# Block-sparse attention and a gated feed-forward on one core: a list-scheduled order, q and k turned by DMA transposes, and a first batch cut into units of 128, 256 and 384 tokens

## The chip, the cores and the metric

The kernel runs on one core of one Trainium2 chip. Times are device microseconds of that core. Every result below is the median of the runs of one kernel, and each was timed against the kernel before in the same rounds on the same chip. One core has no second die to compare with, so a run counts as slow only if it lies more than 1.5% above the fastest of its kernel.

TensorE does the matrix products, VectorE and ScalarE the elementwise work, GpSimd some small work and the loads that change the type on the way, SyncE issues other transfers. A transfer is issued on the queue of one engine and carried out by 16 DMA engines that all queues share.

## The reference

```python
# attention: q, k, v are (4 batches, 8 heads, 768 tokens, 64), float32
scores = scale * np.matmul(q, k.transpose(0, 1, 3, 2))
mask = ...                       # 24 x 24 blocks of 32: window, first and last block, 3 sampled
scores = np.where(mask, scores, -1000000000.0)
attn = softmax(scores)           # cut
x = np.matmul(attn, v)           # then to (3072 tokens, 512)
# feed-forward
xn = x / np.sqrt(np.mean(x * x, axis=-1, keepdims=True) + 1e-06) * rms_g
g, val = xn @ w_gate, xn @ w_val          # 512 -> 1536
out = (g * sigmoid(g) * val) @ w_out      # 1536 -> 512
```

## The kernel before

The mask is added inside the score product. A score tile is the product of 88 rows: 64 of the head, and 24 that select a block of 32 keys and carry the block mask. So `X` holds q and k transposed, with 24 mask rows below them. A pair of heads is one slot of `X`; four pairs make a batch, and each batch is two units of 384 tokens.

```python
    def load_qk(b, lo, hi):                       # casts float32 to bfloat16 on the way
        ...
        nc.gpsimd.dma_start(out=qraw[b][:, lo:hi, :], in_=qv[b, :, lo:hi, :])
        nc.gpsimd.dma_start(out=kraw[b][:, lo:hi, :], in_=kv[b, :, lo:hi, :])

    def transposes(b, pr, early=False):           # 24 for a pair, on TensorE
        ...
        for i, src in enumerate((qraw[b], kraw[b])):
            for c in range(NC):
                for h in range(2):
                    nc.tensor.transpose(
                        out=tt[i][64 * h:64 * h + 64, c * P:(c + 1) * P],
                        in_=src[:, 2 * pr + h, c * D:(c + 1) * D], identity=ident)
        for h in range(2):                        # out of PSUM, on VectorE
            ...
                nc.vector.tensor_copy(
                    out=X[0:D, sl, h], in_=t_[64 * h:64 * h + 64, :, 0:S])

    def ff_g(u, f, wide):                         # gp has one PSUM buffer
        ...
            gp = ps_f.tile([P, TG], FP32, name="gp", tag="gp")
        for c in range(NP):
            nc.tensor.matmul(out=gp, lhsT=wg[...], rhs=xns[u][:, c, :], ...)
        nc.scalar.activation(out=th, in_=gp, func=AF.Tanh, scale=0.5)
        nc.vector.scalar_tensor_tensor(           # uu = (th + 1) * gp frees gp
            out=uu, in0=th, scalar=1.0, in1=gp, op0=ALU.add, op1=ALU.mult)
```

The order of emission comes from a loop over steps. Each step issues one score product and its exp. Other work either has a fixed step or comes from a queue of feed-forward products, paid with credits. Every engine carries out its instructions in the order of emission.

The softmax here doesn't subtract the row's maximum and nothing guards it: scores larger than these inputs give would overflow.

## Time and profile before

| | before |
|---|---|
| median time | 372.5 us |
| TensorE busy | 326.6 us, 88% |
| first score product | 11.1 us |
| first gate product | 52.5 us |

These are lines of the profile's page. The rows of digits divide the span into 40 slices and give the busy tenths of each; PEclk is the clock granted to TensorE in tenths. The queue lines give packets, megabytes and the time that the packets took as a share of all 16 engines' span; q0 is GpSimd's queue, q1 SyncE's. The last two lines are the chain of waits that ended last.

```profile
span 371.2 us, 7228 instructions
...
PE 326.6 (88%) x3074; PEld 197.0 (53%) x3074; DVE 203.0 (55%) x369; ACT 221.8 (60%) x358; POOL 27.4 (7%) x42
...
PE   2768689977989789988999889998999799989995
...
PEclk9999859999999999999999999999999999999999
DMA  6999998006000090006000000000000000000012
...
DMA packets 19877, 21.18 MB, mean 57 GB/s; under 512 B 772, under 2 KB 16644, under 8 KB 19844
...
q0 software_dynamic: 16208, 14.16, 24.6%
q1 hardware_dynamic: 3636, 6.56, 4.9%
...
PE 68%; ACT 15%; DVE 11%; DMA 2%; issue 2%; POOL 1%; DVEq 0%; POOLq 0%
PE gp L297 13%; PE yp L328 13%; PE vp L314 12%; ACT pt L225 6%; ACT sq L253 4%; ACT xn L282 3%; DVE xq L270 3%; DVE uu L303 2%; ACT th L301 2%; DVE X L179 2%; DVE X L182 2%; DMA kb<-in_k_dram 1%; PE tqk L173 1%; DMA out_dram<-yo 1%; PE gw L297 1%
```

TensorE is the limit: it has the most busy time, and 68% of the chain. It is poorly filled only in the first six slices. The DMA engines are nearly full there and almost free afterwards.

The timeline and the groups tell what q and k cost. Columns of the timeline are start, duration, engine, line, operation, output and inputs, count, and in brackets the idle time before it with what ended that. The groups give busy time and mean nanoseconds, then idle time before the group and what ended it.

```profile
6.41 0.85 PE L173 MATMUL tqk<-ident,qb 128*64 128x128 bf16 x12 [6.41 <-DMA qb<-in_q_dram]
...
8.28 1.92 DVE L182 COPY X<-tqk 64x1536 bf16<-64x1536 bf16 x2 [1.49 <-PE tqk L173]
...
11.14 0.82 PE L221 MATMUL s__182<-X 88*128 88x384 bf16 x2 [2.16 <-DVE X L187]
```

```profile
L182 DVE COPY X<-tqk 64x1536 bf16<-64x1536 bf16 x26 | 24.8, 953 | 4.7 <-PE tqk L173 4.5
...
L173 PE MATMUL tqk<-ident,qb 128*64 128x128 bf16 x156 | 7.2, 230 | 6.5 <-DMA qb<-in_q_dram 6.4
```

The first pair's q is in SBUF at 6.4 us and the first score product starts at 11.1 us. A pair costs TensorE 24 transposes at a pitch of 0.033 us, and VectorE two copies of 0.95 us. The Trainium skill (TensorE: Matmul & The Clock Gate, Part 4: PE-mode transpose) gives about 390 ns for a 128x128 transpose in isolation and 275 ns in one kernel. The trace shows less for one of these (230 ns, with 64 columns of the array and not 128), and they overlap: from the start of the first of 24 to the start of the next product it is 0.79 us, so 16 pairs cost 12.7 us and not the 88 that 384 durations of 230 ns would add up to.

In this document "lost" time of TensorE is the length of a window less the products in it times their pitch at full clock (0.1625 us for 128x384, 0.216 for 128x512, 0.033 for a q/k transpose, and so on). A product is counted once, in the window in which it starts, and time at a reduced clock counts as lost in part. Before, that leaves 31.5 us lost up to the first gate product, 11.4 from there to 125 us, 18.8 from 125 to 366, and 4.8 at the end.

### The profile page before, as it was taken

The page shows a single profiled execution, that of the slowest core. Times are in us where ns is not written, and L with a number is a line of the kernel's source. Part 1 is how long each engine was busy: PE and PEld are TensorE (multiplying, and loading weights), DVE is VectorE, ACT ScalarE, POOL GpSimd, SP SyncE. Part 2 cuts the span into 40 slices and gives each one's busy share as a digit, 9 for nine tenths or more (in the row PEclk, how much of TensorE's full clock was granted, in tenths as well). Part 3 has the DMA queues.
Part 4 walks back from the last instruction along what each step waited for, and adds up shares of the span by engine and source line. Part 5 has one row for each costly group of instructions (what it writes and reads, how often), then busy time and mean ns, then how long its engine had stood idle before and what let it go on. Part 6 is the DMA issues. An engine that isn't in the chain of part 4 may idle for free.

```text
span 371.2 us, 7228 instructions
## 1 busy us (share of the span) xinstructions
PE 326.6 (88%) x3074; PEld 197.0 (53%) x3074; DVE 203.0 (55%) x369; ACT 221.8 (60%) x358; POOL 27.4 (7%) x42
## 2 busy tenths in 40 slices
PE   2768689977989789988999889998999799989995
PEld 1345355654656456655666456655666466545552
DVE  4664225666575645655464645665554545476650
ACT  2638947686646756676666766576666866532211
POOL 8520200010000200001000000000000000000000
PEclk9999859999999999999999999999999999999999
DMA  6999998006000090006000000000000000000012
GB/s 95 170 210 208 204 207 129 2 2 87 0 30 30 3 195 4 28 32 86 28 30 4 26 14 18 28 30 3 29 30 29 1 30 28 2 28 31 28 59 86
DMA packets 19877, 21.18 MB, mean 57 GB/s; under 512 B 772, under 2 KB 16644, under 8 KB 19844
## 3 DMA queue, kind: packets, MB, share of 16 engines
q0 software_dynamic: 16208, 14.16, 24.6%
q1 hardware_dynamic: 3636, 6.56, 4.9%
q8 instruction: 24, 0.39, 0.4%
q14 instruction: 9, 0.07, 0.1%
HBM read 28.57 MB, written 6.29 MB: 94 GB/s over the span
## 4 chain that ended last, share of the span: by engine, by line
PE 68%; ACT 15%; DVE 11%; DMA 2%; issue 2%; POOL 1%; DVEq 0%; POOLq 0%
PE gp L297 13%; PE yp L328 13%; PE vp L314 12%; ACT pt L225 6%; ACT sq L253 4%; ACT xn L282 3%; DVE xq L270 3%; DVE uu L303 2%; ACT th L301 2%; DVE X L179 2%; DVE X L182 2%; DMA kb<-in_k_dram 1%; PE tqk L173 1%; DMA out_dram<-yo 1%; PE gw L297 1%
## 5 line engine op out<-in xcount | busy, mean ns | idle before, releaser
L303 DVE SCALAR_TENSOR_TENSOR uu<-th,gp 128x384 bf16<-128x384 bf16 x90 | 49.9, 554 | 82.8 <-ACT th L301 82.3
L297 PE MATMUL gp<-xn,wg 128*128 128x384 bf16 x360 | 73.9, 328 | 5.6 <-DVE uu L303 5.6
L328 PE MATMUL yp<-wo,hp 128*128 128x512 bf16 x288 | 75.9, 379 | 0.0
L314 PE MATMUL vp<-xn,wv 128*128 128x384 bf16 x360 | 73.3, 326 | 0.3 <-DVE hp L317 0.3
L301 ACT ACTIVATE th<-gp 128x384 bf16<-128x384 f32 x90 | 43.9, 487 | 35.9 <-PE gp L297 35.5
L221 PEld LDWEIGHTS <-X 88*128 88x128 bf16 x384 | 36.0, 101 | 43.0 <-issue 13.9
L297 PEld LDWEIGHTS <-wg 128*128 128x128 bf16 x384 | 37.2, 97 | 37.8 <-issue 8.6
L317 DVE TENSOR_TENSOR hp<-uu,vp 128x384 bf16<-128x384 bf16 x90 | 49.9, 554 | 9.3 <-PE vp L314 1.3
L314 PEld LDWEIGHTS <-wv 128*128 128x128 bf16 x384 | 37.0, 97 | 25.2 <-issue 0.8
L238 PEld LDWEIGHTS <-pt 128*128 128x128 bf16 x1152 | 42.5, 100 | 14.0 <-issue 10.8
L328 PEld LDWEIGHTS <-hp 128*128 128x128 bf16 x288 | 27.7, 97 | 24.9
L263 POOL TENSOR_TENSOR rs<-m,nhalf 128x3 f32<-128x3 f32 x8 | 6.9, 865 | 291.5 <-DVE m L260 291.5
L182 DVE COPY X<-tqk 64x1536 bf16<-64x1536 bf16 x26 | 24.8, 953 | 4.7 <-PE tqk L173 4.5
L270 DVE SCALAR_TENSOR_TENSOR xq<-xo,rs,gB 128x512 bf16<-128x512 f32 x24 | 16.6, 747 | 1.6 <-POOL rs L263 1.6
L253 ACT ACTIVATE sq<-xo 128x512 bf16<-128x512 f32 x24 | 14.7, 618 | 2.1 <-DVE xo L244 2.1
L282 ACT COPY xn<-tr 128x1024 bf16<-128x1024 bf16 (+1 forms) x16 | 12.8, 798 | 4.3 <-PE tr L280 4.2
L280 PE MATMUL tr<-ident,xq 128*128 128x128 bf16 x96 | 10.1, 231 | 5.0 <-DVE xq L270 3.7
L337 DVE TENSOR_SCALAR yo<-yp 128x512 f32<-128x512 f32 x21 | 14.4, 685 | 0.1
L173 PE MATMUL tqk<-ident,qb 128*64 128x128 bf16 x156 | 7.2, 230 | 6.5 <-DMA qb<-in_q_dram 6.4
L173 PEld LDWEIGHTS <-qb 128*64 128x64 bf16 x192 | 6.7, 120 | 11.7 <-DMA qb<-in_q_dram 6.4
L280 PEld LDWEIGHTS <-xq 128*128 128x128 bf16 x96 | 6.4, 102 | 12.0 <-DVE xq L270 8.5
L301 ACT ACTIVATE th<-gw 128x384 bf16<-128x384 f32 x6 | 2.9, 490 | 8.8 <-PE gw L297 8.8
(529 smaller groups left out, 409.9 us busy)
## 6 DMA issues: line engine op xcount, KB each, us to landing
out_dram<-yo SPq DMA_DIRECT2D x24, 256.0 KB, 2.0
vr<-in_v_dram POOLq DMA_DIRECT2D x4, 768.0 KB, 8.3
qb<-in_q_dram POOLq DMA_DIRECT2D x3, 768.0 KB, 14.8
kb<-in_k_dram POOLq DMA_DIRECT2D x3, 768.0 KB, 17.7
wg<-in_moe_w_gate_dram POOLq DMA_DIRECT2D x2, 768.0 KB, 17.9
wv<-in_moe_w_val_dram POOLq DMA_DIRECT2D x2, 768.0 KB, 21.4
wo<-in_moe_w_out_dram POOLq DMA_DIRECT2D x1, 1536.0 KB, 32.5
qb<-in_q_dram POOLq DMA_DIRECT2D x2, 192.0 KB, 4.3
```

The source lines that it names most:

```text
L182: nc.vector.tensor_copy(out=X[0:D, sl, h], in_=t_[64 * h:64 * h + 64, :, 0:S])
L221: nc.tensor.matmul(out=s_[:, e, 0:TG], lhsT=X[0:D + NB, sl, e, 1, jt * P:(jt + 1) * P], rhs=X[0:D + NB, sl, e, 0, ic * TG:(ic + 1) * TG], ...
L238: nc.tensor.matmul(out=o_[:, t, e, :], lhsT=pt_[:, jt, e, t * P:(t + 1) * P], rhs=va[:, (2 * pr + e) * NC + jt, 0:D + 1], start=(jt == 0), ...
L253: nc.scalar.activation(out=sq, in_=xo[:, t, :], func=AF.Square, accum_out=ms[:, t:t + 1])
L270: nc.vector.scalar_tensor_tensor(out=xqs[u][:, t, :], in0=xo[:, t, :], scalar=rss[u][:, t:t + 1], in1=gB, op0=ALU.mult, op1=ALU.mult)
L282: nc.scalar.copy(out=xns[u][:, :, lo * P:hi * P].rearrange("p c (t q) -> p t c q", t=hi - lo), in_=tr[:, 0:hi - lo])
L297: nc.tensor.matmul(out=gp, lhsT=wg[:, c, f * P:(f + 1) * P], rhs=xns[u][:, c, :], start=(c == 0), stop=(c == NP - 1))
L301: nc.scalar.activation(out=th, in_=gp, func=AF.Tanh, scale=0.5)
L303: nc.vector.scalar_tensor_tensor(out=uu, in0=th, scalar=1.0, in1=gp, op0=ALU.add, op1=ALU.mult)
L314: nc.tensor.matmul(out=vp, lhsT=wv[:, c, f * P:(f + 1) * P], rhs=xns[u][:, c, :], start=(c == 0), stop=(c == NP - 1))
L317: nc.vector.tensor_tensor(out=hps[u][:, f, :], in0=uu, in1=vp, op=ALU.mult)
L328: nc.tensor.matmul(out=yp, lhsT=hps[u][:, f, t * P:(t + 1) * P], rhs=wo[:, f, :], start=(f == 0), stop=(f == NF - 1))
```

## The change

Its intent is to take 12.7 us of transposes off TensorE and 31 us of copies off VectorE, to reach the feed-forward of the first tokens earlier, and to stall less in between. It does three things at once:

1. q and k are loaded as float32. VectorE casts them into `aug`, a tile whose mask columns are filled once, and one DMA transpose for each pair turns q, k and mask together into `X`.
2. Batch 0 is cut into units of one, two and three tiles of 128 tokens; the others stay at three.
3. The order of emission comes from a list scheduler inside the kernel, with a table of durations.

```diff
+    UNITS = [(0, 0, 1), (0, 1, 2), (0, 3, 3)]
+    UNITS += [(b, c, 3) for b in range(1, B) for c in (0, 3)]
+    aug = [const.tile([P, 2, 2, NC, P], BF16, name=f"aug{i}") for i in range(NAUG)]       # 2
+    X = [const.tile([P, 2, 2, S], BF16, name=f"X{i}") for i in range(NSLOT)]              # 5
+    def load_qk(g):
+        raws[g] = raw.tile([P, 2, 2, NC * D], FP32, name="qk", tag="qk")
+        eng = nc.scalar if b == 0 else nc.sync
+        for i, src in enumerate((qv, kv)):
+            eng.dma_start(out=raws[g][:, i], in_=src[b, :, 2 * pr:2 * pr + 2, :])
...
+    def fill(g):
+        for i in range(2):
+            nc.vector.tensor_copy(out=a[:, i, :, :, 0:D], in_=raws[g][:, i]...)
+    def turn(g):
+        nc.sync.dma_start_transpose(
+            out=X[g % NSLOT].rearrange("p i e (c t) -> p (i e c) t", t=P),
+            in_=aug[g % NAUG].rearrange("p i e c r -> p (i e c r)"))
...
+        op(("ld", g), {"DMA": 2.3}, [], (g if b == 0 else 8.3 + 0.5 * (g - 4),), ...)
+        op(("fill", g), {"DVE": 0.95}, [("ld", g)], (-1 if b == 0 else 4, g), ...)
+        op(("turn", g), {"DMA": 2.5}, [("fill", g)], (-1, g), ...)
...
-    step, credit = 0, 0.0
-    while True:
-        if step < NSTEP:
-            qk_exp(step // NC, step % NC)
...
+    while ready:                      # the earliest start first, then the priority
...
+        end[o["key"]] = fin + LAT[e]
```

In the table a transpose occupies the DMA engines for 2.5 us and is usable 2.0 us later. All 16 are issued on SyncE. The Trainium skill (DMA: Bandwidth & Descriptors, section DMA Transpose (X-bar)) says that two streams transposing at once can corrupt each other.

## The prediction

> **What bounds the kernel now.** TensorE, after a poor start. Pitches from the timeline at full clock: a 128x384 product every 0.1625 us, 128x512 every 0.216, an AV product (65 columns) 0.032, a 128-column transpose 0.033 (q/k) or 0.056 (norm). With the counts of the groups by line: 384 QK = 62 us, 1152 AV = 37, 768 gate/value = 125, 288 output = 62, 96 norm transposes = 5, 384 q/k transposes = 12.7: 304 us of work in a span of 371, 67 lost. Counting products in windows shows where: 0-52.7 us (until the first gate product) holds about 21 us of work, 32 lost; 52.7-100 loses 8; 100-280 loses 16 (91% dense); 280-320 loses 3; 320-362 loses 2; the end 9. In the start ScalarE runs exps back to back at 0.71 us, and the granted clock is 0.5 for about ten us at 43-53.
>
> **What the change does.**
> 1. Removes 384 q/k transposes from TensorE (12.7 us) and their PSUM copies from VectorE (about 31 us: 26 of 0.95, 12 of 0.55). VectorE gets 32 casts of 768 elements; an estimate from the vaug and 0.55 us copies is 0.4-0.9 us each.
> 2. Adds 16 DMA transposes of 786 KB. The Trainium skill (DMA: Bandwidth & Descriptors, Latency and other measured facts) gives 261 GB/s for such transposes: an estimate of 3 us plus a landing of about 2 us (stores land in 2.0 us here). No trace here shows one yet. One per 20 us is needed in steady state, so they hide there; the first four are serial and critical.
> 3. Splits batch 0 into units of 1, 2 and 3 tiles. In the new order about 12 us of TensorE work stands ahead of the first gate product, before 21.
> 4. Replaces the step/credit order by a list schedule with durations close to this trace's (exp 0.715, uu 0.555, pitch 0.1625), which should cut stalls in the middle; the last units' products borrow more PSUM.
> TensorE work becomes about 292 us.
>
> **On the critical path.** The first DMA transpose can't start before load, mask prefill and cast, about 8 us; first QK at about 13 us (before 11.1). Cast loads share the 16 DMA engines with the transposes, 0.9 busy in the first 60 us before, so I expect the fourth pair at about 27 us and the first gate product at 33-36 instead of 52.7: loss about 22. Then until the three-tile feed-forward 8 (clock dip, weights and w_out behind the rsqrt on the GpSimd queue, ScalarE nearly as loaded as TensorE). Steady part, about 228 us of work at 95-96% density: 10. End: 8. Sum 292 + 22 + 8 + 10 + 8 = 340 us.
>
> **Prediction: 340 us, 8 in 10 between 327 and 356.** Faster by over 2%: 0.93; within 2%: 0.05; slower: 0.02.
>
> **What would show each step.** q/k transposes and their copies gone; DMA transposes landing in 4-7 us, the first four finished by 30 us; first gate product at 33-36; density 100-280 at 95% or more; the chain of waits almost wholly TensorE; waits on X only in the first 30 us.
>
> **What would make it wrong.** DMA transposes of 10 us or more: first gate product near 55, time near 355. Fixed order meeting late data: TensorE stalls at its head when a transpose or weight chunk is late; the output product of unit 0, placed early, waits for w_out. SyncE blocking on a transpose delays stores and loads. Density still 91% in the middle: about 350. Clock dip absent or in an idle stretch: 335.

## The result

The changed kernel took 385.8 us (384.0 to 387.0), against 372.6 for the kernel before in the same rounds. All ratios here are the mean time of one kernel's fast runs over the mean of the other's in the same rounds, so not quite the ratio of the medians: 1.035, with a 95% interval of 1.031 to 1.040. It is slower, and its output is correct.

The page of the kernel after, the same lines:

```profile
span 385.2 us, 6892 instructions
...
PE 313.4 (81%) x2838; PEld 198.8 (52%) x2838; DVE 174.3 (45%) x377; ACT 225.2 (58%) x374; POOL 25.1 (7%) x45
...
PE   0007887539759887969998989999999999999995
...
PEclk9999999859998999899998999999999999999999
DMA  6999499999997579920023810000001001001012
...
DMA packets 71988, 40.03 MB, mean 104 GB/s; under 512 B 50836, under 2 KB 68756, under 8 KB 71956
...
q1 hardware_dynamic: 59828, 28.58, 33.1%
q0 software_dynamic: 9952, 7.87, 13.9%
...
PE 61%; DMA 22%; ACT 10%; DVE 3%; SPq 2%; issue 1%; POOL 0%; ACTq 0%
DMA X<-aug 15%; PE gp L299 15%; PE yp L330 14%; PE vp L299 13%; ACT pt L211 6%; DMA qk<-in_k_dram 5%; DMA wo<-in_moe_w_out_dram 2%; ACT sc L246 2%; DVE aug L174 1%; SPq L180 1%; PE tr L277 1%; DVE uu L313 1%; ACT th L307 1%; PE o__862 L225 1%; ACT xn L285 0%
```

TensorE is busy 13 us less, and from the middle on its digits are nearly all nines: the removed work and the better order are both real. But the first three slices are empty and the next ten ragged. The DMA engines stay mostly full up to slice 17 instead of 7. There are 72,000 packets instead of 20,000, 51,000 of them under 512 bytes, and a wait for `X<-aug`, the DMA transpose, is now 15% of the chain.

| TensorE time lost | before | after | the prediction's term |
|---|---|---|---|
| to the first gate product (52.5 and 52.8 us) | 31.5 | 40.6 | 22 |
| from there to 125 us | 11.4 | 29.7 | 8 |
| from 125 us to near the end | 18.8 | 18.0 | 10 |
| end (the last 5 us) | 4.8 | 4.8 | 8 |

The first gate product starts at the same time in both, but in the kernel before, 21.0 us of work had been done by then, and in the changed one only 12.2.

Now the timeline of the start after the change:

```profile
7.08 1.07 POOL L74 DMA_DIRECT2D vr<-in_v_dram  x1
...
8.15 0.77 POOL L164 DMA_DIRECT2D wg<-in_moe_w_gate_dram  x1
...
8.58 30.38 SPq L180 DMA_TRANSPOSE X<-aug  x4
8.90 0.93 POOL L165 DMA_DIRECT2D wv<-in_moe_w_val_dram  x1
...
9.82 1.06 POOL L164 DMA_DIRECT2D wg<-in_moe_w_gate_dram  x1
...
10.87 0.75 POOL L165 DMA_DIRECT2D wv<-in_moe_w_val_dram  x1
...
30.49 0.82 PE L200 MATMUL s__162<-X 88*128 88x128 bf16 x6 [25.22 <-DMA X<-aug]
...
40.84 0.82 PE L200 MATMUL s__277<-X 88*128 88x128 bf16 x6 [1.20 <-DMA X<-aug]
```

The SyncE line merges the first four transposes. The first is issued at 8.6 us, and the product that needs it starts at 30.5: 21.9 us from issue to use. Around it GpSimd issued the loads of v and of two weight chunks, which share the DMA engines with it; by the view by tile a load of v lands after up to 18.3 us and a weight chunk after up to 19.4. From 16 to 30 us the DMA engines moved only 174 to 217 GB/s while fully busy (330 from 8 to 12 us, mostly loads). (Their busy share reads 1.25 to 1.31 there. It sums the times of packets, and above 1 these overlap, so such a sum counts a little too much where several queues are at work.)

The view by tile gives the transposes' time on SyncE's queue (minimum, median, maximum in ns) and their time to landing; the group gives the cast:

```profile
L180 SPq DMA_TRANSPOSE X<-aug x16: 3569/4556/13941, 8.6 to 217.7; - x16
...
DMA to landing us min/median/max: 5.5/7.2/17.9
```

```profile
L174 DVE CAST aug<-qk 128x768 bf16<-128x768 f32 x32 | 17.3, 567 | 54.7 <-DMA X<-aug 36.4
```

Undisturbed, a transpose holds the queue for 3.6 us and lands in 5.5 us. In company it took up to 17.9 us to land by this view, and held the queue, with everything behind it, up to 13.9 us. (The view finds a landing for 14 of the 16 transposes only, and the first is not among them, so its maximum stays below the 21.9 us above. The packets in the trace show it: those of the first transpose run from 12.7 to 29.4 us, and other transfers moved 2.7 MB in between.) The cast itself is cheap, 0.57 us.

The later stop, at 73 to 83 us, is a chain that must be read across engines:

```profile
62.43 13.17 SPq L180 DMA_TRANSPOSE X<-aug  x1
...
75.65 0.58 SPq L70 DMA_DIRECT2D qk<-in_q_dram  x1
...
81.39 0.56 DVE L174 CAST aug<-qk 128x768 bf16<-128x768 f32 x1 [10.06 <-DMA qk<-in_q_dram]
...
82.92 0.28 DVE L313 SCALAR_TENSOR_TENSOR uu<-th,gp 128x128 bf16<-128x128 bf16 x1
...
83.25 0.58 PE L299 MATMUL gp<-xn,wg 128*128 128x128 bf16 x4 [10.16 <-DVE uu L313]
```

The fifth transpose holds SyncE from 62.4 to 75.6 us, beside the loads of w_out and of the next v. Behind it on SyncE stand the loads of the next pairs; the first is issued at 75.65. VectorE has reached the cast of that pair and stands 10.1 us there. Behind the cast in VectorE's order stands `uu`, which would free the one PSUM buffer of the gate product, and TensorE waits 10.2 us for it. The label on TensorE's wait says VectorE; the cause is a transpose on a queue two steps further back. The same happens once more at 115.6 us (4.7 us).

### The profile page after: what moved, and what is told of

Same layout as the page of the kernel before. It is cut to its first block, busy times and chain, and to the rows that moved or that the text cites. A ratio compares the mean times of both kernels' runs of the same rounds, so it can differ in the third digit from the quotient of the medians.

```text
span 385.2 us, 6892 instructions
## 1 busy us (share of the span) xinstructions
PE 313.4 (81%) x2838; PEld 198.8 (52%) x2838; DVE 174.3 (45%) x377; ACT 225.2 (58%) x374; POOL 25.1 (7%) x45
## 3 DMA queue, kind: packets, MB, share of 16 engines
q0 software_dynamic: 9952, 7.87, 13.9%
## 4 chain that ended last, share of the span: by engine, by line
PE 61%; DMA 22%; ACT 10%; DVE 3%; SPq 2%; issue 1%; POOL 0%; ACTq 0%
DMA X<-aug 15%; PE gp L299 15%; PE yp L330 14%; PE vp L299 13%; ACT pt L211 6%; DMA qk<-in_k_dram 5%; DMA wo<-in_moe_w_out_dram 2%; ACT sc L246 2%; DVE aug L174 1%; SPq L180 1%; PE tr L277 1%; DVE uu L313 1%; ACT th L307 1%; PE o__862 L225 1%; ACT xn L285 0%
## 5 line engine op out<-in xcount | busy, mean ns | idle before, releaser
L299 PE MATMUL gp<-xn,wg 128*128 128x384 bf16 (+2 forms) x432 | 78.4, 313 | 23.6 <-DVE uu L313 23.4
L313 DVE SCALAR_TENSOR_TENSOR uu<-th,gp 128x384 bf16<-128x384 bf16 (+2 forms) x108 | 54.8, 508 | 79.5 <-ACT th L307 77.6
L307 ACT ACTIVATE th<-gp 128x384 bf16<-128x384 f32 (+2 forms) x108 | 49.2, 456 | 57.5 <-PE gp L299 56.6
L299 PE MATMUL vp<-xn,wv 128*128 128x384 bf16 (+2 forms) x432 | 78.8, 314 | 2.9 <-DVE hp L321 2.9
L321 DVE TENSOR_TENSOR hp<-uu,vp 128x384 bf16<-128x384 bf16 (+2 forms) x108 | 53.0, 507 | 13.4 <-PE vp L299 9.9
L174 DVE CAST aug<-qk 128x768 bf16<-128x768 f32 x32 | 17.3, 567 | 54.7 <-DMA X<-aug 36.4
L339 ACT ACTIVATE yo<-yp 128x512 f32<-128x512 f32 x20 | 11.9, 597 | 25.7 <-PE yp L330 25.1
L260 POOL TENSOR_TENSOR rs<-m,nhalf 128x3 f32<-128x3 f32 (+2 forms) x9 | 7.3, 813 | 236.3 <-DVE m L253 236.1
L246 ACT ACTIVATE sc<-xo 128x512 bf16<-128x512 f32 x24 | 14.8, 620 | 1.9 <-DVE xo L237 1.9
L285 ACT COPY xn<-tr 128x1536 bf16<-128x1536 bf16 (+2 forms) x9 | 11.7, 1302 | 4.9 <-PE tr L277 4.9
## 6 DMA issues: line engine op xcount, KB each, us to landing
qk<-in_q_dram SPq DMA_DIRECT2D x12, 384.0 KB, 5.2
qk<-in_k_dram SPq DMA_DIRECT2D x12, 384.0 KB, 5.8
vr<-in_v_dram POOLq DMA_DIRECT2D x4, 768.0 KB, 11.3
qk<-in_q_dram ACTq DMA_DIRECT2D x4, 384.0 KB, 7.1
qk<-in_k_dram ACTq DMA_DIRECT2D x4, 384.0 KB, 7.8
wg<-in_moe_w_gate_dram POOLq DMA_DIRECT2D x4, 384.0 KB, 11.0
wv<-in_moe_w_val_dram POOLq DMA_DIRECT2D x4, 384.0 KB, 12.6
```

The lines of the kernel that those rows point to most:

```text
L174: nc.vector.tensor_copy(out=a[:, i, :, :, 0:D], in_=raws[g][:, i].rearrange("p h (c d) -> p h c d", d=D))
L246: nc.scalar.activation(out=sc, in_=xos[u][:, t].rearrange("p h d -> p (h d)"), func=AF.Square, accum_out=mss[u][:, t:t + 1])
L299: nc.tensor.matmul(out=p_, lhsT=w_[:, c, f * P:(f + 1) * P], rhs=xns[u][:, c, :], start=(c == 0), stop=(c == NP - 1))
L307: nc.scalar.activation(out=t_, in_=tiles["gp", u, f], func=AF.Tanh, scale=0.5)
L313: nc.vector.scalar_tensor_tensor(out=t_, in0=tiles.pop(("th", u, f)), scalar=1.0, in1=tiles.pop(("gp", u, f)), op0=ALU.add, op1=ALU.mult)
L321: nc.vector.tensor_tensor(out=hps[u][:, f, :], in0=tiles.pop(("uu", u, f)), in1=tiles.pop(("vp", u, f)), op=ALU.mult)
```

## The experiments

The theory: the list schedule and the small units pay as intended, and the loss is the DMA transposes', in two ways. They take far longer beside other transfers (the start), and they hold SyncE and then VectorE, in order, while they do (60 to 125 us). Rivals: the new order itself is bad, since it meets late data with a fixed order; or the small units cost more than they give; or it is the transposes' sheer DMA time, whatever stands beside or behind them.

### e1_gate: the first transposes without company

```diff
+    def gate(g):                     # GpSimd reads one element of X[g]: it stands until g is turned
+        nc.gpsimd.tensor_copy(out=gscr, in_=X[g][0:1, 0, 0, 0:2])
     def load_v(b):
+        if b == 0: gate(2)
...
     def load_w(i):
+        if i == 0: gate(3)
```

> The changed kernel, order of all engines kept, with two one-element GpSimd copies that read X: the load of v waits for the third DMA transpose, the weight loads for the fourth. Theory (the first transposes are slow because v and weight loads share the DMA engines): the first transpose lands by 15 us instead of 30.5, the fourth by 30 instead of 40.8, the first gate product comes at 38-43 instead of 52.75, time 372-378. Rival (the first transposes are slow by themselves, set-up or 256-byte packets): the first still lands near 30, the weights come later still, time 395 or more.

Measured: 385.9 us, ratio 1.033 (1.029 to 1.036), no gain. Of the timeline, the first score product and the first product with v:

```profile
19.45 0.82 PE L209 MATMUL s__163<-X 88*128 88x128 bf16 x6 [14.19 <-DMA X<-aug]
...
38.81 0.82 PE L234 MATMUL o__230<-vaug,pt 128*128 128x65 bf16 x12 [12.81 <-DVE vaug L194]
```

The first product came 11 us earlier, so other loads had indeed held up the first transposes. But v, held back, landed late, and the product with v waited 12.8 us. First gate product 52.4 us, as before the edit. The wait moved from X to v: in either of these two orders the DMA engines had too much to do in the first 50 us (e8 below has a third order, and it does better). The time of 372 to 378 us was missed.

### e2_ldfirst: the loads of the next pairs ahead of the transposes

```diff
-        op(("ld", g), {"DMA": 2.3}, [], (g if b == 0 else 8.3 + 0.5 * (g - 4),), ... at=1.0)
+        op(("ld", g), {"DMA": 2.3}, [], (g if b == 0 else -2,), ... at=1.0 if b == 0 else 40.0)
```

> The changed kernel with the q/k loads of batches 1 to 3 placed ahead of the fifth and later transposes on SyncE's queue. Theory (loads stand behind a blocked transpose, the cast on VectorE waits for them and holds up uu behind it, which holds TensorE): the TensorE gaps of 10.2 us at 73-83 and 4.7 us at 111-116 go, time 370-377. Rival (the loads are late because the DMA engines are full, whatever the order): a gap of 5 us or more stays in 70-120, time within 4 us of 385. The start is as before the edit: first gate product at 52-54.

Measured: 370.0 us, ratio 0.991 (0.989 to 0.994), as expected. The 10.2 us gap became 3.1; what is lost between first gate product and 125 us fell from 29.7 to 21.9, and after 125 us from 18.0 to 9.9. The start is as it was (first score product 30.4). So SyncE's order alone was worth 16 us, and with it the change is no slower than before, but no faster by 2% either. A 4.6 us gap at 111 us remains, behind a cast that waits for a buffer of `aug` whose transpose held SyncE for 11.6 us.

### e3_both: both edits

The edits of e1 and e2 together.

> Both edits. If the two losses are separate, the gains add: 357-366 us. If they are one loss (DMA time), the second edit adds under 4 us to the first.

Measured: 372.6 us, ratio 0.999 (0.994 to 1.004). Missed: the effects don't add, and the sum is worse than e2 alone. Held loads of v now meet the earlier loads of the next pairs, and the product with v stands 14.6 us at 42 us.

### e4_pe_turn: the new order and units, the old way of turning q and k

```diff
-        raws[g] = raw.tile([P, 2, 2, NC * D], FP32, name="qk", tag="qk")
+        raws[g] = raw.tile([P, 2, 2, NC * D], BF16, name="qk", tag="qk")   # cast by the load
-        eng = nc.scalar if b == 0 else nc.sync
+        eng = nc.gpsimd
...
-        nc.sync.dma_start_transpose(...)
+                    nc.tensor.transpose(...)          # 24 for a pair, into PSUM tile "s"
+            nc.vector.tensor_copy(out=X[g % NSLOT][0:D, :, h, :], in_=t_[...])
...
-        op(("turn", g), {"DMA": 2.5}, ...)
+        op(("fill", g), {"PE": 0.8}, ...)
+        op(("turn", g), {"DVE": 1.92}, ...)
```

> One part of the change undone: the list schedule and the units of 1, 2 and 3 tiles stay, but q and k come by casting loads, are transposed on TensorE (12.7 us more of it) and copied by VectorE into tiles whose mask rows are filled once. Theory (the DMA transposes carry the loss): no TensorE gap over 4 us after the first QK, first gate product at 35-42, time 345-358. Rival (the fixed order or the small units carry it): 368 or more.

Measured: 353.7 us, ratio 0.947 (0.945 to 0.949), as expected. Its chain of waits:

```profile
PE 76%; DVE 6%; issue 6%; ACT 5%; POOL 4%; DMA 2%; POOLq 0%; ACTq 0%
```

The granted clock of the profiled run was 1.00 from 32 us on, where its record begins. First score product 17.6, first gate product 40.1; after that no wait of TensorE over 1.9 us, and 4.5 us lost after 125 us. The rival "the new order itself is bad" falls. TensorE has some 12.8 us more counted work than in the changed kernel, and 46.0 us less lost.

### e5_dma_in_old: the DMA transposes in the old order

```diff
-    def transposes(b, pr, early=False): ...            # TensorE and PSUM copies, mask rows
+    def transposes(b, pr):                             # casting loads kept
+            nc.vector.tensor_copy(out=a[:, i, :, :, 0:D], in_=src[...])
+        nc.sync.dma_start_transpose(out=X[g % NSLOT]..., in_=a...)
...
-        at(6 * (pr - 1) + 3, 0.95, transposes, 0, pr, True)
+        at((0, 0, 2, 5)[pr], 0, transposes, 0, pr)
```

> One part of the change alone: the kernel before, its step/credit order, its casting loads of whole batches and its units of 384, but the TensorE transposes and their copies replaced by VectorE fills of mask-prefilled tiles and 16 DMA transposes on SyncE, issued one pair earlier than before. Theory (the transposes' own time on the shared DMA engines costs the start, whatever the order): first QK near 30 us, first gate product at 68 or later, time 382-400. Rival (only the new order of queues made them costly; here the loads lie far ahead): the start loses under 8 us, TensorE saves 12.7, time 364-375.

Measured: 405.6 us, ratio 1.087 (1.081 to 1.092), and even worse than expected. The first score product came at 20.8 us, earlier than the expected 30, but the next pairs were late. Here the loads keep their cast, and SyncE issues only two small loads and the stores beside the transposes, yet TensorE stood 21.8 us for `X` at 47 us and the first gate product came at 98. A transpose held SyncE for up to 19.2 us and landed in up to 29.4. The DMA transposes lose time in both orders.

### e6_units384: e4 with whole units

```diff
-    UNITS = [(0, 0, 1), (0, 1, 2), (0, 3, 3)]
-    UNITS += [(b, c, 3) for b in range(1, B) for c in (0, 3)]
+    UNITS = [(b, c, 3) for b in range(B) for c in (0, 3)]
```

> The TensorE-transpose version of the list schedule (e4) with all units of 384 tokens. If small first units are worth something: first gate product at 47-52 instead of 40.1, time 358-365 against 353.7. If the list schedule fills the start as well without them: within 2 us of 353.7.

Measured: 359.0 us, ratio 0.963 (0.958 to 0.969), the time as expected. The first gate product came at 62.5 us, not at the expected 47 to 52: a reminder that this moment is a poor measure. In this run TensorE did more of the attention first and lost only 4.5 us from there to 125 us. The small units give 5 us; the rival that they cost more than they give falls.

### e7_half: transposes of half the size (the result is wrong on purpose)

The edit of e2, and only the k half of `aug` is transposed; the q half of `X` is filled once with a constant.

```diff
+    for x in X:
+        nc.vector.memset(x[:, 0], 0.01)
...
-            out=X[g % NSLOT].rearrange(...), in_=aug[g % NAUG].rearrange(...))
+            out=X[g % NSLOT][:, 1].rearrange(...), in_=aug[g % NAUG][:, 1].rearrange(...))
```

> Wrong result on purpose: e2 with the DMA transpose of K only (12 of 24 blocks, half the bytes); the Q half of X is set once to a constant. Theory (DMA engine time bounds the start and 60-120 us): the fourth pair is there by 32 us, first gate product at 43-47 instead of 52.7, gaps of 3.1 and 4.6 us at 80 and 111 under 2 us, time 352-361. Rival (a fixed cost per transpose or a queue wait): first gate product at 50 or later, time 366 or more.

Measured: 352.8 us against 370.0 for e2, ratio to before 0.946 (0.944 to 0.948); the relative error of 1.1 is intended. Half the bytes are worth 17 us. Half transposes hold SyncE for a median 2.1 us and land in 3.6 to 11.3 (median 4.3), and no gap of TensorE after the first gate product exceeds 1.7 us. The first gate product came at 47.9 us, just past the expected 43 to 47. (The fills delay the first transpose from 8.6 to 15.5 us, so the gain in the start is understated.) With the number of the transposes and their place in the order kept, less transposing is less loss. Not all of the 17 us need be DMA time: q is a constant here, and the clock cost 1.7 us in its record against 5.9 in e2's, which can be the effect of fewer stops or of the data; no run tells which.

The run also gives the price. The lines of SyncE's queue in e2 and in e7:

```profile
q1 hardware_dynamic: 59828, 28.58, 33.4%
```

```profile
q1 hardware_dynamic: 35252, 22.29, 24.9%
```

The two differ by 16 half transposes and nothing else: 33.4% of 16 engines' 369.2 us is 123.3 us, 24.9% of 350.9 is 87.4. The difference over 16 is 2.24 us for a half, so by this estimate (the other packets of that queue may have changed a little too) 4.5 us of all 16 engines for a whole transpose of 786,432 bytes: 175 GB/s. The packets say the same more directly. In the changed kernel's trace 49,152 packets of 256 bytes on this queue are the 16 transposes, 3072 each. Their times sum to 80.5 us of all 16 engines, 5.0 for a transpose on average: about 4.1 for those with nothing beside them (198 to 202 GB/s moved in three such windows), 6.2 and 6.4 for the two that met large loads.

### e8_gate_w: e2, with only the weights held back

```diff
     def load_w(i):
+        if i == 0: gate(3)            # v is not held
```

> e2, with only the weight loads (not v) held until the fourth transpose has landed. Theory in its first form (weights slow the transposes; without them the start is quick): first QK at 20-25, first gate product at 45-49, time 362-367. Rival (the start is bound by the sum of the DMA work, so order only moves the wait): first gate product within 2.5 us of 52.7, time 368-374.

Measured: 363.5 us, ratio 0.976 (0.971 to 0.980), as expected. First score product 21.2, first gate product 45.1. So the order was worth another 6.5 us against e2 (of other rounds), and the rival, that order only moves the wait, does not hold. This is the best order found with all 16 transposes on the DMA engines; some 23 us are still lost from there to 125 us.

### e9_start: e4, with the start of the old kernel

```diff
-    for g in range(NRAW):
-        load_qk(g)
+    load_qk(0)                        # the others after the mask constants
...
+        if 0 < g < NSLOT:
+            mask_rows(g)              # at first use, not all five ahead of the first product
```

> A version meant to beat both: the list schedule with TensorE transposes (e4), its start in the order of the kernel before: first pair's load, then the constants, then the other loads; mask rows of a slot filled at its first use. First QK at 11-13 us instead of 17.6. If the late start is on the bound path: 348-351 us. If TensorE makes it up later: 352.5-355.

Measured in five rounds: 350.9 us (350.1 to 351.4), ratio 0.940 (0.938 to 0.942), correct, as expected. It beats both kernels. Its page:

```profile
PE   1679879997999999999999999999999999999995
...
PEclk9999989999999999999999999999999999999999
DMA  5997999898001333200000001001000100010022
...
PE 80%; DVE 5%; issue 5%; ACT 4%; POOL 3%; DMA 2%; POOLq 0%; ACTq 0%
```

The first score product is back at 10.4 us, and 80% of the chain is TensorE; no DMA wait of weight is left in it.

### e10_all_dma: e8, with the casts moved to GpSimd

```diff
-            nc.vector.tensor_copy(
+            (nc.vector if g < NP else nc.gpsimd).tensor_copy(     # batches 1 to 3
```

w_out is loaded with the last chunk of weights.

> The best of the DMA transpose path: loads ahead on SyncE's queue, weights held until the fourth transpose, casts of batches 1 to 3 on GpSimd, w_out issued with the last weight chunk. If the gains add: 354-360 us, still above the TensorE transposes at 353.7. If DMA time bounds the first 120 us whatever the queues: 361-366.

Measured: 365.0 us, ratio 0.979 (0.976 to 0.982). Missed; the rival held, and it is no faster than e8. `uu` no longer stands behind a cast, but TensorE now waits 2.6 us for X itself, 4.0 for v and 3.5 for the normalization, which stands on GpSimd behind the casts.

### e11_fill_pool: the changed kernel with its casts on GpSimd

The same edit on the changed kernel, with both halves of w_out at the place of the first.

> The changed kernel; the casts of batches 1 to 3 into the prefilled tiles go to GpSimd in the same places of the order (both w_out loads are issued ahead of them), everything else is kept. Theory (the cast, waiting for its load, holds up uu behind it on VectorE and so TensorE): the gaps of 10.2 us at 73-83 and 4.7 us at 111-116 fall under 3 us, time 372-380. Rival (the transposed tile itself is late, so TensorE stops anyway at the next QK): gaps of the same size on X, time 382-388.

Measured: 382.7 us, ratio 1.023 (1.017 to 1.029). Missed: 3 us of gain where 6 to 14 were expected. The stop at 73 to 83 us is gone, which fits the chain read above (w_out moved too, so the cast is not the only difference). But the same late data now holds GpSimd, and with it the normalization and the load of v:

```profile
94.62 1.93 PE L278 MATMUL tr<-ident,xq 128*128 128x128 bf16 x12 [7.06 <-DVE xq L268]
...
106.01 2.13 PE L226 MATMUL o__1150<-vaug,pt 128*128 128x65 bf16 x36 [6.47 <-DVE vaug L186]
```

A 7.1 us wait for `xq` and 6.5 us for `vaug` took its place, and another 5.9 us for `xq` at 168 us. Changing the engine that stands in the queue moved the wait and did not remove it.

### e12_hybrid: e9, with 12 of the 16 transposes on the DMA engines

Batch 0 is turned on TensorE; batches 1 to 3, where the DMA engines should be freer, by DMA, with casting loads.

```diff
+        if b:
+            op(("cast", g), {"DVE": 0.55}, [("ld", g)], (4, g), ...)
+            op(("turn", g), {"DMA": 2.5}, [("cast", g)], (-1, g), ...)
+            continue
```

> e9 with the transposes of batches 1 to 3 (12 of 16 pairs) moved to DMA transposes from mask-prefilled tiles; batch 0 stays on TensorE, all loads stay casting loads on GpSimd's queue, so the first transpose comes after the start. TensorE loses 12 x 0.79 = 9.5 us of work, VectorE some 20 us. Theory (a DMA transpose costs nothing once the start and the weight loads are over): 341-347 us against 350.9, no TensorE gap over 2 us. Rival (5 us of DMA time each and the casts waiting on VectorE's queue still hold TensorE while v, w_out and q/k of batch 1 load): gaps of 2 us and more between 60 and 130, 349-358.

Measured in five rounds, one slow run (369.6 us) left out: 362.1 us, ratio 0.969 (0.966 to 0.971); 11 us slower than e9. Missed: the saved TensorE time (12 x 0.79 = 9.5 us) was more than lost. The rival's direction held, and the loss exceeded its range. Lines of the page and of the timeline:

```profile
q0 software_dynamic: 18656, 14.16, 28.4%
q1 hardware_dynamic: 40884, 15.99, 20.7%
...
PE 72%; DMA 15%; ACT 6%; DVE 4%; issue 1%; POOL 1%; DVEq 0%; SPq 0%; ACTq 0%; POOLq 0%
PE gp L337 16%; PE yp L368 16%; PE vp L337 15%; DMA X<-aug 15%; ACT pt L249 4%; PE tqk L197 2%; PE tr L315 1%; DVE aug L204 1%; ACT sc L284 1%; DVE uu L351 1%; PE o__1258 L263 1%; DVE X L219 1%; DVE yo L379 0%; PE o__2182 L263 0%; POOL qk L71 0%
```

```profile
56.08 23.58 SPq L210 DMA_TRANSPOSE X<-aug  x2
...
79.18 0.63 DVE L204 COPY aug<-qk 128x768 bf16<-128x768 bf16 x2 [5.97 <-DMA X<-aug]
...
82.87 1.01 PE L337 MATMUL gp<-xn,wg 128*128 128x256 bf16 x4 [7.99 <-DVE uu L351]
```

Two transposes hold SyncE for 23.6 us, VectorE stands at a cast for a free `aug`, `uu` behind it, and TensorE stands 8.0 us: the same chain as in the changed kernel, without its slow start. It gives the price a second time: 20.7% of 360.7 us less e9's 5.1% of 349.4 is 56.8 us of all 16 engines, 4.7 us for each of the 12 transposes. That is an average of unlike ones: in the windows of four late transposes with nothing beside them the engines moved 254 to 271 GB/s, more than the 198 to 202 of the changed kernel. No run tells why the two differ.

## Why the prediction was wrong

It said 340 us, with 327 to 356; the result was 385.8.

**Right.** The work left for TensorE, "about 292 us", is 292.2 in the counts. The casts (0.57 us, estimated 0.4 to 0.9) and the 12 us of work ahead of the first gate product (12.2) were right, and so was "the first four are serial and critical". The list schedule "should cut stalls in the middle": with it and TensorE transposes 3.1 to 4.5 us are lost after 125 us (e6, e4), where the kernel before lost 18.8.

**The failed step is the second: "an estimate of 3 us plus a landing of about 2 us".** As the time of one transpose alone, 5 us was nearly right: 5.5 measured (4.5 in e12). As a cost it was wrong in three ways, and the rest of the prediction stood on it.

1. *The rate.* The estimate took 261 GB/s from the Trainium skill (DMA: Bandwidth & Descriptors, Latency and other measured facts), the lower of the two rates there. Undisturbed transposes of e12 reached it, those of the changed kernel came to about 200, and over a whole run the engine time is 4.5 (e7) to 5.0 us (the packets of the changed kernel), some 160 to 175 GB/s. Sixteen transposes are 72 to 80 us of all 16 engines where the prediction's 3 us make 48, nine of them in the first 125 us, beside the loads (28.6 MB in the whole run).
2. *The sharing.* "I expect the fourth pair at about 27 us and the first gate product at 33-36": the first pair alone came at 30.5, the fourth at 40.8, the first gate product at 52.8. The same page of the skill, section Issuing engines are not separate DMA queues, says that transfers from different engines run on the same 16 DMA engines and interleave. The trace agrees: with other loads held (e1) the first product starts at 19.5 us, with only the weights held (e8) at 21.2, otherwise at 30.5. The prediction named the sharing and gave it no time: from the first product at 13 us to the fourth pair at 27 it allowed 4.7 us for each of three transposes, what one takes alone. This term was 22 us and measured 40.6.
3. *The queue.* "One per 20 us is needed in steady state, so they hide there." They don't come one per 20 us: five are issued between 62 and 107 us, with their loads beside w_out and v, and a transpose that is late keeps SyncE, then the loads behind it, then the casts on VectorE and `uu`, then TensorE. The prediction listed "SyncE blocking on a transpose" as a risk, but gave it 8 us with everything else in that stage; 29.7 were lost. Loads put ahead (e2) gave 16 us back, half of them before 125 us and half after.

The prediction also wrote, under what would make it wrong, "DMA transposes of 10 us or more: first gate product near 55, time near 355". The condition came true for three of the 16 (the first, the second and the fifth) and the gate time was right (52.8), but the price was not: it let slow transposes cost only the start, and so left out the third point.

**The sum.** Lost beyond the terms: start 18.6, next stage 21.7, after 125 us 8.0, end 3.2 less; with 0.2 of difference in the work count that is, but for rounding, 45.2 us, the miss of the profiled run (385.2 less 340).

**The parts of the change, as the runs show them.** The list schedule with whole units and TensorE transposes, and with its loads by pairs, is worth 13.7 us (372.7 of its rounds to 359.0). The small units add 5.3 (e4). The DMA route for q and k, against e4, costs 32.1 us (385.8 less 353.7): in the profiled runs it saves 12.8 us of TensorE work and loses 46.0. All three compare medians of different rounds, some on different chips, and are good to about 1 us. The 32.1 is for the route as a whole, with its float32 loads, mask columns and queues, not for the transpose instruction alone; e12, which keeps the casting loads and the fast start, still loses 11 us against e9 by the transposes of batches 1 to 3.

**Open.** The granted clock fell to half in the changed kernel from 75 to 88 us and in some later places, and the lost clock, weighted by TensorE's busy time, is 7.7 us in that run's record, 4.2 before, none in e4's. The Trainium skill (TensorE: Matmul & The Clock Gate, Why this matters for your kernels) advises against idle gaps over about 3 us between matmuls, and the dip at 75 us does begin 1.8 us into the 10.2 us stop. But e6 shows more (12.8 us, in its start) and is fast, and no run changes the clock alone. Nor do the records cover the same stretch: they begin at 44 us in the changed kernel, 27 before, 32 in e4 and 14 in e6, and the products ahead of them are slow as well (in e4 four 256-column score products take 1.04 us at 30.5 us and 0.60 at 33.9). So perhaps 3 us of the loss against the kernel before is the clock's; this is argued and not shown. Also open is how well a schedule would do that knows the real cost: with 5 us for a transpose in its table, the list scheduler found no ready operation that could start and stopped (no run shows it; the kernel's own scheduling code, run again, does), and no such kernel ran.

## What to carry to other kernels

Cost a transfer twice before moving work onto it: its engine time among everything else that the DMA engines must carry in that stage, and its time at the head of the queue that issues it, because what stands behind it there waits too. When an in-order engine stops for late data, look at what stands behind it; moving the stop to another engine (e10, e11), or another transfer to the front (e1), can just move the wait. A better order took off 16 us (e2) and 6.5 more (e8), but only less work in that stage (e7, e4) took off most of the rest. A bundled change should be tried in parts: two of these three were worth 19 us, and the one that looked like saved work cost 32, more than both.

## What the Trainium skill lacked or had wrong

- DMA: Bandwidth & Descriptors, Latency and other measured facts: 261 GB/s for DMA transposes with a non-contiguous middle dimension, more for a contiguous case. Here transposes of 786,432 bytes from SBUF to SBUF, in packets of 256 bytes, with nothing beside them moved 254 to 271 GB/s in e12, as the page says, but only 198 to 202 in the changed kernel, and over a whole run they cost 4.5 to 5.0 us of all 16 engines, some 160 to 175 GB/s. Alone one landed in 5.5 us (4.5 in e12). The page has no figure for transposes beside other loads: here the last packet of the first came 20.8 us after its issue in the changed kernel, and one landed after 29.4 us in e5.
- The same page, Issuing engines are not separate DMA queues: the time to initiate a transfer "is usually small relative to the DMA itself". That held for loads (0.37 to 0.58 us of the queue, up to 1.1 in company). It did not for transposes: 3.6 us of the queue alone, 13.9 at most in the changed kernel and 19.2 in e5, during which nothing behind could be issued. The page counts the sequencer's cycles for a transpose only in a comparison made for another chip; no page has this time as measured on this one.
- TensorE: Matmul & The Clock Gate, Part 4: PE-mode transpose: it gives durations (390 and 275 ns) and no pitch. Back to back, 24 transposes of a 128x64 block took 0.79 us, 0.033 us each, and that, with two copies of 0.95 us on VectorE, is the figure to set against a DMA transpose.
